# Two edits to DMA issue order in a fused spectral-filter and GEGLU kernel: the first gate weights move to ScalarE's queue, and the two returns of the third group part are issued together

## The chip, the core and the metric

The kernel runs on one core of a Trainium2 chip. The metric is device time in microseconds (us), the median over runs of the whole program. A profiled execution has a time of its own, and its trace covers a span a little shorter than that time.

## The reference

The input x has shape 1 x 2048 x 512 in bf16. It is normalised row by row, and two branches work on the result:

```python
xn = _layernorm(x, axis=-1)
return x + _A_ref(xn, A_w_r, A_w_i) + _B_ref(xn, B_w_gate, B_w_up, B_w_down)

# _A_ref: irfft2(rfft2(xn) * (w_r + 1j * w_i))          (2048 x 257 filter)
# _B_ref: (gelu(xn @ w_gate) * (xn @ w_up)) @ w_down     (512 -> 1792 -> 512)
```

## The kernel before

**Tiling.** The 2048 rows are held as 16 tiles of 128 rows by 512 columns. Row block b (0 to 3) is four tiles. Everything is on the chip at once: weights, filters and activations have their own SBUF buffers, and each engine has one list of instructions, written out by hand in program order by `sch.op`. An instruction waits on semaphores of what it depends on; an engine never goes past an instruction that waits. So the order of the calls at the end of the function is the order of each engine's work. A DMA is issued by the engine whose list holds it: `load(..., eng="sp")` puts it on SyncE (SP), `eng="act"` on ScalarE (ACT). In the profile, SP's DMAs run on queue q1 and ACT's on queue q10.

**GEGLU.** `geglu_unit(b, fc, a, w)` multiplies one 128-column slice of the gate weights (4 matmuls, line 547), then the same slice of the up weights (4 matmuls, line 547), applies gelu on ACT (line 559) and the product on VectorE (line 567). `down_unit` does the 14 matmuls of the down projection (line 593) for one tile and adds to x (line 604). These units are also the filler that is put between the steps of the spectral branch so that TensorE (PE) has work while the spectral branch waits for transfers.

**The start.** SP issues, in this order, tiles x0 and x1 (128 KB each, lines 363-364), the first piece of gate and up weights (384 KB each, `load_w(0)`, line 365: called wg0 and wu0 here), tiles x2 and x3, the second piece of gate and up weights (256 KB each, wg1 and wu1, line 368), and the rest. ACT's first instruction is the load of a 32 KB identity matrix (line 344). Then tiles 0 and 1 are normalised: on VectorE the statistics of tile 0 (lines 413, 414), those of tile 1, the reciprocal for tile 0 (line 423) and its normalisation (line 436), in that order; the square roots are on ACT (line 419). PE transposes the normalised tile with the identity (line 451), VectorE copies it back (line 457), and the first gate matmul follows.

**The spectral branch.** Its two FFT directions are matmuls with constant matrices. In the middle, the 32 frequency groups go through 16 units u of two groups: `unit_B(u)` transforms (line 695), `product(u)` applies the filter, `unit_c(u)` transforms back (line 726), ACT copies the result from PSUM to a buffer Vp (line 731), and SP stores it in the DRAM buffer stage_g (line 735, 128.5 KB). SP also issues, for each u, two 64 KB copies JX (line 703). The groups fall into four parts of four units. When a part is stored, `back(part, pq, eng)` (line 738, DMA at line 743) reads it back in another layout, in two returns pq = 0 and 1 of 256 KB each:

```python
if u in (9, 10, 13, 14, 17, 18):
    back(u // 4 - 2, (u - 9) % 4, "act")
```

So parts 0, 1 and 2 (the first three) are returned by ACT, one return in step u and the other in step u + 1; part 3 is returned by SP after the loop (line 911), when the last stores have landed. In step 18, `unit_c(14)` and `unit_c(15)` come before the second return of part 2. `unit_e(j)` (line 757), the first step of the last transform, waits for all eight returns (`spec["perm2"]`). Its PE instructions are behind the filler of line 912. After it, `unit_fin(j)` finishes each tile on PE, ACT, VectorE and GpSimd (POOL, lines 792 and 796), and SP stores it.

Of the kernel before, what the change touches and what calls it, by code (L numbers as in the profile page):

```python
# [17 lines left out]
P = 128  # L18
# [133 lines left out]
class _Sched:  # L152
# [14 lines left out]
    def total(self, stream):  # L167
        return (stream, self.stream_cnt[stream])
# [59 lines left out]
def bass_parallel_sum__spectral_gfnet__glu_gated_geglu__prompt_kernel(  # L228
# [11 lines left out]
    c_small = nc.inline_tensor(small_np, name="c_small")  # L240
# [9 lines left out]
    with ExitStack() as es:  # L250

        def sb(name, shape, dt=BF16):
            return es.enter_context(nc.sbuf_tensor(name, shape, dt))
# [13 lines left out]
        small = sb("small", [P, small_np.shape[1]])  # L267
# [30 lines left out]
        ident = small[:, 0:P]  # L298
# [40 lines left out]
        def load(stream, dst, src, eng="sp"):  # L339
            sch.op(eng, lambda e: e.dma_start(dst, src), stream=stream)  # L340
            return total(stream)


        ev_id = load("ident", small[:, 0:P], c_small.ap()[:, 0:P], eng="act")
        WPIECES = ((0, 384), (384, 640), (640, 896), (896, 1280), (1280, FF))
        ev_w = {}
        spec = {}
# [1 line left out]
        def load_w(i, which=(0, 1), eng="sp"):  # L349
            a, b = WPIECES[i]  # L350
            for q in which:
                dst, src = ((wg_sb, B_w_gate), (wu_sb, B_w_up))[q]
                name = "w%d%s" % (i, "gu"[q])
                load(name, dst[:, :, a:b], src[:, a:b].rearrange("(r p) f -> p r f", p=P), eng=eng)
                ev_w[i, q] = total(name)
# [4 lines left out]
                ev_x[j] = ev  # L360

        ev_x = {}
        for j in (0, 1):
            ev_x[j] = load("x%d" % j, x_sb[:, j, :], xv[:, j, :])
        load_w(0)
        for j in (2, 3):
            ev_x[j] = load("x%d" % j, x_sb[:, j, :], xv[:, j, :])
        load_w(1)
# [318 lines left out]
        def unit_B(u):  # L687
            s3 = u % 4
            slot, bdeps = ring_sp.alloc(2)

            def f_b(e):
                ins = None
                for i in range(2):
                    g = 2 * u + i
                    ins = e.matmul(sp_bank(slot + i)[:, 0:NK], BM[:, 1 if g == 0 else 0, :], Tp[:, g, :], start=True, stop=True)  # L695
                return ins

            ev_p = sch.op("pe", f_b, deps=[spec["perm1"], ev_small] + bdeps)
            spec["B_last"] = ev_p
            ev_Xc[u] = sch.op("act", lambda e: e.activation(Xc[s3], sp_pair(slot), ACT.Copy), deps=[ev_p] + Xc_readers[s3])  # L700
            ring_sp.add_reader(slot, ev_Xc[u], 2)
            for h in range(2):
                sch.op("sp", lambda e, h=h: e.dma_start(JX[s3][64 * h:64 * h + 64, :, :], Xc[s3][64 - 64 * h:128 - 64 * h, :, :]),
                       deps=[ev_Xc[u]] + JX_readers[s3], stream="jx%d" % s3)
            ev_JX[u] = total("jx%d" % s3)
            Xc_readers[s3] = [ev_JX[u]]

        def product(u):

            s2, s3 = u % 2, u % 4  # L710
            gs = slice(2 * u, 2 * u + 2)
            a = sch.op("dve", lambda e: e.tensor_tensor(M1[s2], Xc[s3], wr_sb[:, gs, :], ALU.mult), deps=[ev_Xc[u]] + M_readers[s2] + spec["wr"])
            b = sch.op("dve", lambda e: e.tensor_tensor(JX[s3], JX[s3], wi_sb[:, gs, :], ALU.mult), deps=[ev_JX[u], spec["neg"][u // 4]])
            ev_Y[u] = sch.op("dve", lambda e: e.tensor_tensor(M1[s2], M1[s2], JX[s3], ALU.add), deps=[a, b])
            Xc_readers[s3].append(a)
            JX_readers[s3] = [ev_Y[u]]

        def unit_c(u):
            s2, sv = u % 2, u % 3
            slot, bdeps = ring_sp.alloc(2)  # L720

            def f_c(e):
                ins = None
                for i in range(2):
                    kind = 1 if 2 * u + i == 0 else 0
                    ins = e.matmul(sp_bank(slot + i)[:, 0:NK], CM[:, kind, :], M1[s2][:, i, :], start=True, stop=True)  # L726
                return ins

            ev_p = sch.op("pe", f_c, deps=[ev_Y[u]] + bdeps)
            M_readers[s2] = [ev_p]  # L730
            ev_v = sch.op("act", lambda e: e.activation(Vp[sv][:], sp_pair(slot), ACT.Copy), deps=[ev_p] + Vp_readers[sv])  # L731
            ring_sp.add_reader(slot, ev_v, 2)
            part = next(i for i, (lo, hi) in enumerate(PARTS) if lo <= 2 * u < hi)
            name = "vd%d_%d" % (part, sv)
            sch.op("sp", lambda e: e.dma_start(d2[2 * u:2 * u + 2].rearrange("g r k -> r g k"), Vp[sv][:]), deps=[ev_v], stream=name)
            Vp_readers[sv] = [total(name)]

        def back(part, pq, eng):

            lo, hi = PARTS[part]  # L740
            src = bass.AP(tensor=d2.tensor, offset=d2.offset + (lo * P + 16 * pq) * NK + pq,
                          ap=[[32 * NK, 4 * (hi - lo)], [NK, NJ], [1, HD]])
            sch.op(eng, lambda e: e.dma_start(V[4 * lo:4 * hi, :, pq * HD:(pq + 1) * HD], src),
                   deps=[total("vd%d_%d" % (part, i)) for i in range(3)] + [spec["A_last"]], stream="perm2")
            spec["perm2"] = total("perm2")
# [104 lines left out]
        def filler(n=1):  # L850
            for _ in range(n):
                u = next(fill, None)
                if u is None:
                    return
                todo["left"] -= 1
                if u[0] == "g":
                    geglu_unit(u[1], u[2])
                else:
                    down_unit(u[1], u[2])
# [36 lines left out]
        for u in range(19):  # L896
            for v in ((14, 15) if u == 18 else (u - 4,)):
                if v >= 0:
                    unit_c(v)
            if u < 16:  # L900
                unit_B(u)
            for v in {15: (12, 13), 16: (14,), 17: (15,), 18: ()}.get(u, (u - 3,)):
                if v >= 0:
                    product(v)
            if 1 <= u < 18:
                filler()

            if u in (9, 10, 13, 14, 17, 18):
                back(u // 4 - 2, (u - 9) % 4, "act")
        for pq in range(2):  # L910
            back(3, pq, "sp")
        filler(todo["left"] - 15 - 2)
# [59 lines left out]
```

## Time and profile before

| what | us |
|---|---|
| median of 3 runs | 182.88 |
| lowest and highest run | 182.47, 183.36 |
| the profiled execution: its time | 182.96 |
| the profiled execution: its span | 181.2 |
| PE busy | 174.0 (96% of the span) |
| VectorE, ACT, POOL busy | 116.1, 87.4, 55.3 |
| granted TensorE clock | 1.0 throughout |

Times inside the profile are us from the start of the span. The 1.76 us between span and time lie outside of what the trace shows. A group of instructions is named by engine, line, operation and tile. SPq and ACTq are the issuing of DMAs by these engines; the time to landing of a DMA runs from its issue to its semaphore.

### The profile page before, as it was taken

Reading aid. Unit: us, or ns where it says so; the run is one execution under the profiler, and the core shown is the slowest. Engines: PE = TensorE matmul, PEld = TensorE weight load, DVE = VectorE, ACT = ScalarE, POOL = GpSimd, SP = SyncE. Lnnn points to the kernel's source line nnn. Section 1 sums busy time; section 2 is a strip of 40 time slices with the busy share of each in tenths; the row PEclk is TensorE's granted clock in tenths of the full one; section 3 lists DMA queues with packets and bytes.
Section 4 is the critical chain, followed back from the end, with each engine's and each line's share of the span. In section 5 each row is a group of like instructions: output and inputs, shape, how many; then the busy total and the mean of one; then the engine's idle time right before and its main releaser. Section 6 shows DMA issues by size and latency. Waiting matters only on the chain.

```text
span 181.2 us, 3209 instructions
## 1 busy us (share of the span) xinstructions
PE 174.0 (96%) x1163; PEld 98.1 (54%) x1163; DVE 116.1 (64%) x255; ACT 87.4 (48%) x164; POOL 55.3 (31%) x54
## 2 busy tenths in 40 slices
PE   7899999999999999999999999999799999999991
PEld 7678655555555544454554555454255555555550
DVE  3587977788765636537586858863336678873372
ACT  3744347776562533166374737362154366642300
POOL 0047262344560000000000000000006979995663
PEclk9999999999999999999999999999999999999999
DMA  5999999999997794813343866754500111111001
GB/s 136 324 339 381 373 358 167 182 183 225 219 200 196 151 271 141 261 36 84 92 122 83 195 154 134 188 92 113 119 0 29 55 35 58 58 60 62 31 29 58
DMA packets 37520, 27.15 MB, mean 150 GB/s; under 512 B 6656, under 2 KB 36736, under 8 KB 37376
## 3 DMA queue, kind: packets, MB, share of 16 engines
q1 hardware_dynamic: 34192, 25.34, 55.1%
q10 hardware_dynamic: 3312, 1.61, 4.8%
q8 instruction: 9, 0.15, 0.3%
q14 instruction: 7, 0.06, 0.2%
HBM read 17.48 MB, written 6.30 MB: 131 GB/s over the span
## 4 chain that ended last, share of the span: by engine, by line
PE 68%; POOL 13%; DMA 9%; DVE 3%; issue 3%; SPq 2%; POOLq 1%; ACT 1%; ACTq 0%; DVEq 0%
PE ps L547 41%; PE ps L593 17%; POOL x_sb L796 7%; POOL bufC L792 5%; DMA wu_sb<-in_B_w_up_dram 3%; DMA stage_g<-Vp 3%; DMA bufB<-stage_g 3%; PE ps L646 2%; PE ps L620 2%; PE ps L695 2%; PE ps L726 2%; SPq L340 2%; DVE bufC L789 1%; DVE bufC L788 1%; PE ps L757 1%
## 5 line engine op out<-in xcount | busy, mean ns | idle before, releaser
L547 PE MATMUL ps<-xnT,wu_sb 128*128 128x512 bf16 (+2 forms) x264 | 59.2, 347 | 0.4 <-DMA wu_sb<-in_B_w_up_dram 0.4
L547 PE MATMUL ps<-xnT,wg_sb 128*128 128x512 bf16 (+2 forms) x264 | 59.2, 347 | 0.4 <-DVE xnT L457 0.4
L567 DVE TENSOR_TENSOR hT<-ps,gg 128x512 bf16<-128x512 f32 (+2 forms) x66 | 39.5, 606 | 27.1 <-PE ps L547 25.3
L593 PE MATMUL ps<-wd_sb,hT 128*128 128x512 bf16 (+2 forms) x238 | 50.8, 366 | 0.0
L559 ACT ACTIVATE gg<-ps 128x512 bf16<-128x512 f32 (+2 forms) x66 | 35.1, 533 | 26.5 <-PE ps L547 22.7
L792 POOL TENSOR_TENSOR bufC<-bufC 128x256 bf16<-128x256 f32 x16 | 14.8, 922 | 89.9 <-DVE bufC L789 89.9
L547 PEld LDWEIGHTS ps<-xnT,wu_sb 128*128 128x128 bf16 x264 | 24.9, 98 | 24.6 <-DMA wu_sb<-in_B_w_up_dram 0.9
L593 PEld LDWEIGHTS ps<-wd_sb,hT 128*128 128x128 bf16 x238 | 22.4, 98 | 23.0
L547 PEld LDWEIGHTS ps<-xnT,wg_sb 128*128 128x128 bf16 x264 | 23.8, 98 | 15.2 <-issue 0.7
L604 DVE TENSOR_TENSOR x_sb<-ps,x_sb 128x512 bf16<-128x512 f32 (+2 forms) x17 | 11.1, 660 | 24.3 <-PE ps L593 16.0
L796 POOL TENSOR_TENSOR x_sb<-x_sb,bufC 128x512 bf16<-128x512 bf16 x16 | 18.7, 1170 | 2.3
L507 POOL TENSOR_TENSOR bufC<-bufA 128x1024 bf16<-128x1024 bf16 x8 | 16.8, 2125 | 8.5 <-DVE bufA L436 8.5
L762 ACT ACTIVATE bufA<-ps 128x512 bf16<-128x512 f32 x16 | 9.4, 597 | 17.2 <-PE ps L757 17.2
L731 ACT ACTIVATE Vp<-ps 128x514 bf16<-128x514 f32 x16 | 9.5, 600 | 15.3 <-PE ps L726 15.3
L654 ACT ACTIVATE bufB<-ps 128x512 bf16<-128x512 f32 x16 | 11.9, 745 | 9.5 <-PE ps L646 9.5
L413 DVE BATCH_NORM_STATS2 st<-x_sb 128x6 f32<-128x512 bf16 x16 | 10.9, 680 | 2.2 <-DMA x_sb<-in_A_x_dram 2.2
L788 DVE TENSOR_TENSOR bufC<-bufC,ps 128x256 f32<-128x256 f32 x16 | 6.7, 419 | 4.6 <-ACT bufC L785 4.6
L627 ACT ACTIVATE tmp<-ps 128x512 bf16<-128x512 f32 x9 | 5.4, 598 | 6.1 <-PE ps L620 6.1
L428 POOL TENSOR_SCALAR rstd<-ag 128x4 f32<-128x4 f32 (+1 forms) x4 | 1.3, 317 | 21.3 <-DVE ag L414 21.3
L700 ACT ACTIVATE Xc<-ps 128x514 bf16<-128x514 f32 x12 | 7.0, 595 | 1.0 <-PE ps L695 1.0
L757 PEld LDWEIGHTS ps<-fa,bufB 128*128 128x128 bf16 x64 | 4.8, 98 | 5.1 <-DMA bufB<-stage_g 1.8
L757 PE MATMUL ps<-fa,bufB 128*128 128x128 bf16 x64 | 6.0, 219 | 1.3 <-DMA bufB<-stage_g 1.3
(50 smaller groups left out, 138.2 us busy)
## 6 DMA issues: line engine op xcount, KB each, us to landing
stage_g<-Vp SPq DMA_DIRECT2D x16, 128.5 KB, 3.4
bufC<-stage_p SPq DMA_DIRECT2D x4, 512.0 KB, 5.2
out_dram<-x_sb SPq DMA_DIRECT2D x15, 128.0 KB, 1.7
wd_sb<-in_B_w_down_dram SPq DMA_DIRECT2D x1, 1792.0 KB, 14.6
stage_p<-bufB SPq DMA_DIRECT2D x7, 256.0 KB, 5.6
wr_sb<-in_A_w_r_dram SPq DMA_DIRECT2D x6, 257.0 KB, 10.5
wi_sb<-in_A_w_i_dram SPq DMA_DIRECT2D x6, 257.0 KB, 10.1
JX<-Xc SPq DMA_DIRECT2D x24, 64.2 KB, 2.4
```

The source lines that it names most:

```text
L413: ev = sch.op("dve", lambda e: e.bn_stats(st[:, j, :], x_sb[:, j, :]), deps=[ev_x[j]])
L507: ev_hf[m] = [sch.op("pool", lambda e, t=t, op=op: e.tensor_tensor(half[:, m, t, :, :], rows[:, 0, :, :], rows[:, 1, :, :], op), deps=deps ...
L547: ins = e.matmul(gu_bank(slot)[:, 0:w], wsb[:, dc, fc * P:(fc + 1) * P], xnT[:, dc, b * 512 + a:b * 512 + a + w], start=(dc == 0), stop=(d ...
L559: ev_gg = sch.op("act", lambda e: e.activation(gg, gu_bank(gslot)[:, 0:w], ACT.Gelu_apprx_tanh), deps=[ev_gm] + gg_readers[s2])
L567: ev_h = sch.op("dve", lambda e: e.tensor_tensor(hT[hb][:, fc, a:a + w], gu_bank(uslot)[:, 0:w], gg, ALU.mult), deps=[ev_um, ev_gg] + hdeps)
L593: ins = e.matmul(bank(slot)[:, 0:w], hT[hb][:, fc, jj * P:(jj + 1) * P], wd_sb[:, fc, cs], start=(fc == 0), stop=(fc == NFC - 1))
L604: ev_a = sch.op("dve", lambda e, slot=slot, cs=cs, w=w: e.tensor_tensor(x_sb[:, j, cs], bank(slot)[:, 0:w], x_sb[:, j, cs], ALU.add), deps ...
L654: ev_T[j] = sch.op("act", lambda e: e.activation(dst, src, ACT.Copy), deps=[ev_p])
L731: ev_v = sch.op("act", lambda e: e.activation(Vp[sv][:], sp_pair(slot), ACT.Copy), deps=[ev_p] + Vp_readers[sv])
L757: ins = e.matmul(sp_bank(slot)[:, ci * P:(ci + 1) * P], V[:, j, V0[ci]:V0[ci] + HD - 1:2], EM[:, j, :], start=True, stop=True)
L792: y = [sch.op(("dve", "pool")[h], lambda e, h=h, op=op: e.tensor_tensor(rS[s2][:, h * HD:(h + 1) * HD], yeS[s2][:, 0, :], yeS[s2][:, 1, :] ...
L796: ev_o = sch.op("pool", lambda e: e.tensor_tensor(x_sb[:, j, :], x_sb[:, j, :], rS[s2], ALU.add), deps=[a, b, ev_xn[j]] + ev_acc.get(j, []))
```

## The change

There are two edits. First, wg0 is issued by ACT as its first instruction, ahead of the identity, and is gone from SP's list; wu0 stays on SP and follows x1 directly. Second, both returns of part 2 are issued by ACT in step 17, one behind the other, instead of one in step 17 and one in step 18. The other returns stay where they were. No other instruction changes its place on its engine. The code below the first edit stands one line lower than before.

```diff
-        ev_id = load("ident", small[:, 0:P], c_small.ap()[:, 0:P], eng="act")
...
         ev_x = {}
+        load_w(0, (0,), eng="act")
+        ev_id = load("ident", small[:, 0:P], c_small.ap()[:, 0:P], eng="act")
         for j in (0, 1):
             ev_x[j] = load("x%d" % j, x_sb[:, j, :], xv[:, j, :])
-        load_w(0)
+        load_w(0, (1,))
...
-            if u in (9, 10, 13, 14, 17, 18):
-                back(u // 4 - 2, (u - 9) % 4, "act")
+            for pq in {9: (0,), 10: (1,), 13: (0,), 14: (1,), 17: (0, 1)}.get(u, ()):
+                back(u // 4 - 2, pq, "act")
```

## The prediction

> **What bounds the kernel now.** I read the page's busy times first, then PE's waits over the whole span, then the chain of waits around the two edits, and last the packets of each DMA queue in short windows.
>
> ```profile
> PE 174.0 (96%) x1163; PEld 98.1 (54%) x1163; DVE 116.1 (64%) x255; ACT 87.4 (48%) x164; POOL 55.3 (31%) x54
> ```
>
> PE is the bound. A change that leaves PE's instructions alone can only move where PE stands idle, so the list of PE's waits is the list of what there is to win:
>
> ```profile
> PE ps L757 <- DMA bufB<-stage_g: 1.3, 1, 1.3
> PE ps L527 <- DVE hT L407: 1.0, 1, 1.0
> PE ps L547 <- DMA wu_sb<-in_B_w_up_dram: 0.4, 2, 0.2
> PE ps L547 <- DVE xnT L457: 0.4, 1, 0.4
> PE ps L451 <- DVE rstd L423: 0.2, 1, 0.2
> ```
>
> The columns are total us, times, longest. One wait of 1.3 us is for the returns. Two waits of 0.2 us are for up weights at the start. The rest belongs to the start-up chain from tile 0. Between 13 and 130 us PE waits for nothing, so what shifts PE at the start shifts everything behind it. The chain of waits around the returns, in order of time (start, us, what):
>
> ```profile
> 120.57 0.56 ACT Vp L731
> ...
> 121.14 5.28 DMA stage_g<-Vp
> ...
> 126.43 0.33 SPq L743
> ...
> 126.81 4.58 DMA bufB<-stage_g
> ...
> 131.43 0.62 PE ps L757 x8
> ```
>
> The last store of stage_g takes 5.28 us to land; SP then issues the last two returns, and PE starts 4.6 us after that. PE's last filler ends at 130.15, hence 1.28 us idle. From 131.43 to the end PE, VectorE and POOL follow one another in PE's rhythm of 2.17 us a tile (1.73 + 0.22 + 0.22 in the chain), so an earlier start there is kept to the end.
>
> **Second edit (returns).** Why does that store take 5.28 us, when those issued at 93.33, 95.50 and 115.46 land in 2.7 to 2.8? Packets by queue (q1 is SP, q10 is ACT) in two windows, 120.2 to 122.8 and 122.8 to 125.2:
>
> ```profile
> q10 hardware_dynamic: 691, 0.35, 91.1%
> ```
>
> ```profile
> q1 hardware_dynamic: 544, 0.26, 41.9%
> q10 hardware_dynamic: 321, 0.16, 21.8%
> ```
>
> A return is 528 packets. The two last stores, issued at 120.65 and 121.14, move no packet until 122.8. At that point ACT has moved 796 - 528 = 268 packets of the second return, issued at 120.26. So a transfer on the other queue, if issued behind a return, starts when about half of the return has moved. The second return itself begins badly: from 121.2 to 121.6 the core moves 20 to 31 GB/s.
>
> After the edit ACT issues the second return at 119.26, right behind the first (118.95 to 119.26, 0.31 us an issue). It does not have to wait, since part 2's stores have landed by 116.8. Behind it on ACT are the two Vp copies, which wait for PE until 120.03; the second issue ends at 119.57, so it delays nothing. The first return is half through at 120.8, as now. The pair needs 528 packets more until it is half through its second. In 120.6 to 121.0 the returns move 189 packets, some 450 per us, so that point comes 1.15 us later, at 121.95. The stores then start 0.85 us sooner than 122.8, which moves PE's start up by as much. Bounds: PE's idle time caps the gain at 1.28 us. A store that met no return would take 3.0 us at most (91.16) and land at 124.1, well beyond the cap. At the other end, a slow first half (2.5 us from issue, as the second return had) puts the same point at 118.95 + 2.5 + 1.15 = 122.6, and only 0.2 is won. A loss is excluded, because no instruction comes later on any engine. I take 1.05, the middle between 0.85 and the cap: the last two returns on SP, issued 0.38 us apart (126.43 and 126.81), had moved 746 of 1056 packets 2.77 us after the first issue, here 121.7, so the point of 796 may come a little before 121.95.
>
> **First edit (weights).** What it removes: SP's issue of wg0, 0.43 us with its gap 0.47 us. wu0 and all of SP's later loads are issued 0.47 us sooner. What it can give is PE's two waits for up weights, 0.24 us at 6.84 and 0.18 at 10.31. The transposes of tiles 2 and 3 at 12.63 came ready within 0.1 us of PE, behind VectorE work that shares only the first gain, so I count 0.24 to 0.42 and take 0.35. ACT's list: the identity moves back by one issue, the table load of 1.28 us (now 1.18 to 2.46) ends some 0.4 us later, and the first square root at 4.06 covers it. The identity now queues behind 384 KB; wg0 on SP has all its packets through 3.1 us after issue, so on ACT by about 3.8, the identity lands before 5, and PE first needs it at 5.43. wg0 itself (now landing at 5.54, used at 6.21) comes sooner.
>
> What it costs is x0 and x1, which now share the start with 384 KB. VectorE's rows show when they are needed:
>
> ```profile
> 3.11 0.69 DVE L413 BATCH_NORM_STATS2 st<-x_sb 128x6 f32<-128x512 bf16 x1 [2.19 <-DMA x_sb<-in_A_x_dram]
> 3.84 0.18 DVE L414 BATCH_NORM_AGGREGATE ag<-st 128x2 f32<-128x6 f32 x1
> 3.94 0.66 DVE L413 BATCH_NORM_STATS2 st<-x_sb 128x6 f32<-128x512 bf16 x1
> ...
> 4.74 0.13 DVE L423 RECIPROCAL rstd<-rstd 128x1 f32<-128x1 f32 x1
> ```
>
> VectorE starts when x0 lands, and x1 (landing at 3.37) has until 3.9 before it too delays the reciprocal and with it the first matmul. The nearest row for an SP transfer beside a large ACT transfer is JX beside a return, ACT issue at 109.41, SP issue at 109.44 (windows 109.42 to 112.0, then 112.0 to 112.8):
>
> ```profile
> q10 hardware_dynamic: 278, 0.14, 44.4%
> q1 hardware_dynamic: 273, 0.13, 18.6%
> ```
>
> ```profile
> q10 hardware_dynamic: 232, 0.11, 53.0%
> q1 hardware_dynamic: 141, 0.10, 41.7%
> ```
>
> The 273 of q1 are an older store; JX has its first packet at 112.0, after 278 packets of the return, and lands in 4.0 us where 2.0 to 2.4 is usual. wg0 too is 528 packets. Half of them have moved 1.85 (first return of part 2) to 2.5 us (wg0 on SP, the return at 109.41) after the issue; from 0.73 that is 2.6 to 3.25.
>
> x1 is issued at 1.17, clearly behind wg0. It starts at 2.6 to 3.25, takes 0.8 us for its 136 packets beside wg0's second half (141 packets of q1 in 0.8 us above) and lands 0.55 us after the last, at 3.95 to 4.6. That is 0 to 0.7 us too late, and I take 0.35. x0 is issued at 0.72, wg0 at 0.73. If x0 goes first it lands as now; the edit then costs 0.35 and gives 0.35, sum 0 (-0.4 to +0.4).
>
> Sum: 182.96 (span 181.2 + 1.76) - 1.05 + 0 = 181.9. The median of the runs is 0.08 below the profiled time.
>
> **A rule against the first edit.** The rows above show no exchange of packets between the queues in the first half of a large transfer. The Trainium skill, "DMA: Bandwidth & Descriptors", section "Issuing engines are not separate DMA queues", says that DMAs from different engines run on the same 16 engines and interleave, so that issuing from several saves only issue time. As an estimate from that page, interleaving from the first packet on would put 104 KB of wg0 between x0's packets and as much again between x1's, about 0.3 us each at some 320 GB/s, which also ends near 181.9.
>
> **The rivals.** (1) x0 goes behind wg0. Its lead is 0.01 us, and now the identity, issued at 0.73, has 26 packets through before x0's second. Then x0 starts at 2.6 to 3.25, needs 0.8 and 0.55 and lands at 3.95 to 4.6 instead of 3.11. That is 0.85 to 1.5 us, middle 1.15, less 0.35: +0.8, and 182.96 - 1.05 + 0.8 = 182.7. For it speaks JX, 0.03 us behind a return; against it, that x0 is first by the issue rows. (2) Slower: x0 waits for all of wg0, not half. wg0 has its last packet 3.1 us after issue, at 3.8; x0 alone then needs 0.45 and 0.6 and lands at 4.85, 1.75 late. Less 0.35 that is +1.4, and 183.3; if the returns give only 0.2, 184.2. It decides from an x0 landing past 3.11 + 0.35 + 1.05 = 4.5. Against it: JX went through after half. (3) The second edit does not do what it says: the stores land as late as now for another reason, since the last packet at 125.1 precedes the landing by 1.3 us. Then 0 to 0.2 is won, and with x0 first the time is 182.9.
>
> **How the numbers follow.** The forecast has 0.53 (its own range 181.3 to 182.4), rival 1 has 0.29 (182.0 to 183.3), rival 2 has 0.10, rival 3 has 0.08. The range 181.2 to 183.5 leaves out the worse half of rival 2 and corners of the others. A measurement here tells about 0.5% from no change, 0.91 us, so faster means below 181.97. About 0.38 of the forecast's 0.53 lies there and 0.04 of rival 1. Slower means above 183.8: 0.07 of rival 2, 0.04 of rival 1's upper end with weak returns, 0.01 else. Faster 0.42, same 0.46, slower 0.12.
>
> **What would show it.** Right: q1 has its first store packets at about 122 in place of 122.8, the last store lands in under 4.5 us, and PE's wait at line 758 shrinks from 1.3 to under 0.4. At the start VectorE's first statistics begin near 3.1, the second near 4.2, and PE's waits for wu_sb are gone. Wrong: first statistics after 3.8 (rival 1) or 4.5 (rival 2), or a last store still near 5 us (rival 3).

## The result and the profile after

In this measurement the changed kernel is slower. Its median is 184.17 us (183.11 to 185.62, 13 runs) against 182.88 us (182.15 to 183.40, 13 runs) before. The ratio is 1.0073, with a 95% interval of 1.0044 to 1.0103. That is above the range's upper end of 183.5. The kernel was measured twice more in the experiments below (both_again, both_third), and there its medians, 182.25 and 182.24 us, lie inside the range and can't be told from the kernel before.

The profiled execution of the changed kernel took 183.5 us, with a span of 181.7 us (before: 181.2). Its busy times hardly differ from before, so the half microsecond in this execution is idle time of PE. All lines of the code below the first edit have moved down by one. PE's waits (total us, times, longest):

```profile
PE ps L758 <- DMA bufB<-stage_g: 1.0, 1, 1.0
PE ps L528 <- DVE hT L408: 1.0, 1, 1.0
PE ps L528 <- DVE rstd L424: 0.5, 1, 0.5
PE ps L548 <- DVE xnT L458: 0.4, 1, 0.4
```

The waits for wu_sb are gone, as forecast. The wait for the returns fell only from 1.3 to 1.0 us. The third line is new: PE's warm-up matmuls are over, and PE stands still until tile 0 is ready. VectorE's rows at the start show why (start, us, what, idle time before and its releaser):

```profile
3.20 0.69 DVE L414 BATCH_NORM_STATS2 st<-x_sb 128x6 f32<-128x512 bf16 x1 [2.29 <-DMA x_sb<-in_A_x_dram]
...
5.13 0.69 DVE L414 BATCH_NORM_STATS2 st<-x_sb 128x6 f32<-128x512 bf16 x1 [1.02 <-DMA x_sb<-in_A_x_dram]
```

x0 came in time (3.20; before 3.11). x1 did not. The second statistics start at 5.13 instead of 3.94, and the reciprocal, the normalisation and the first transpose stand behind them. The transposes of tile 2, after which PE no longer waits for this chain, start at 13.44 instead of 12.63. So 0.81 us of the 1.19 us is still there, and stays to the end. The chain of waits around the returns (start, us, what):

```profile
121.95 4.37 DMA stage_g<-Vp
...
126.34 0.33 SPq L744
...
126.71 5.20 DMA bufB<-stage_g
...
131.95 0.62 PE ps L758 x8
```

The last store landed in 4.37 us instead of 5.28, as the second edit intended. But the last returns themselves took 5.20 us instead of 4.58. PE starts line 758 at 131.95, before at 131.43: 0.52 us later, which is the difference of the spans: 0.81 us from the start, less some 0.3 us of wait.

What one profile does not show is the clock. The mean granted clock of the 13 runs of the changed kernel is under 0.992 in six (184.17 to 185.62 us) and from 0.995 to 1.0 in the other seven (median 183.5 us). Of the 122 runs of the kernel before that accompany the experiments, one is under 0.992.

### The profile page after: what moved, and what is told of

Its sections match the earlier page's. It is cut to its first block, busy times and chain, and to the rows that moved or that the text cites. A ratio compares the mean times of both kernels' runs of the same rounds, so it can differ in the third digit from the quotient of the medians.

```text
span 181.7 us, 3190 instructions
## 1 busy us (share of the span) xinstructions
PE 173.4 (95%) x1144; PEld 98.7 (54%) x1163; DVE 116.2 (64%) x255; ACT 87.3 (48%) x164; POOL 55.3 (30%) x54
## 4 chain that ended last, share of the span: by engine, by line
PE 67%; POOL 13%; DMA 7%; DVE 6%; issue 3%; ACT 1%; POOLq 1%; SPq 0%; DVEq 0%
PE ps L548 40%; PE ps L594 17%; POOL x_sb L797 7%; POOL bufC L793 5%; DMA bufB<-stage_g 3%; DMA stage_g<-Vp 2%; DMA x_sb<-in_A_x_dram 2%; PE ps L647 2%; PE ps L621 2%; PE ps L696 2%; PE ps L727 2%; DVE st L414 1%; DVE bufC L790 1%; DVE bufC L789 1%; PE ps L758 1%
## 5 line engine op out<-in xcount | busy, mean ns | idle before, releaser
L548 PE MATMUL ps<-xnT,wg_sb 128*128 128x512 bf16 (+2 forms) x254 | 57.5, 345 | 0.9 <-DVE xnT L458 0.4
L594 PE MATMUL ps<-wd_sb,hT 128*128 128x512 bf16 (+2 forms) x232 | 50.0, 366 | 0.3
L414 DVE BATCH_NORM_STATS2 st<-x_sb 128x6 f32<-128x512 bf16 x16 | 10.9, 682 | 3.3 <-DMA x_sb<-in_A_x_dram 3.3
L786 ACT ACTIVATE bufC<-ps 128x256 f32<-128x256 f32 x16 | 6.0, 378 | 2.6 <-PE ps L779 2.6
```

The source lines that it names most:

```text
L414: ev = sch.op("dve", lambda e: e.bn_stats(st[:, j, :], x_sb[:, j, :]), deps=[ev_x[j]])
L548: ins = e.matmul(gu_bank(slot)[:, 0:w], wsb[:, dc, fc * P:(fc + 1) * P], xnT[:, dc, b * 512 + a:b * 512 + a + w], start=(dc == 0), stop=(d ...
L594: ins = e.matmul(bank(slot)[:, 0:w], hT[hb][:, fc, jj * P:(jj + 1) * P], wd_sb[:, fc, cs], start=(fc == 0), stop=(fc == NFC - 1))
```

## The experiments

My first theory was: x1's late landing costs about 0.8 us, and a pause of PE that now follows the warm-up lets the clock drop in some executions. The rivals were ScalarE's queue itself (the issue, the later table load, the later identity) and the returns, which won less than forecast. Ratios are to the kernel before, run on the same chip in the same series, with 95% intervals.

### One edit at a time

weights_only has the first edit alone; the returns are as before:

```diff
-            for pq in {9: (0,), 10: (1,), 13: (0,), 14: (1,), 17: (0, 1)}.get(u, ()):
-                back(u // 4 - 2, pq, "act")
+            if u in (9, 10, 13, 14, 17, 18):
+                back(u // 4 - 2, (u - 9) % 4, "act")
```

> Only the first edit: wg0 on ScalarE as its first instruction, the returns as before. Theory T (x1 queues behind wg0, lands near 5.1 instead of 3.4, and PE's start-up chain is late by about 1.2 us less the 0.42 us of up-weight waits): slower than before by 0.8 us at least, near 184, with the second VectorE statistics starting near 5.1 and PE's wait for the returns still 1.3 us. Rival R1 (the returns edit is what costs): 182.9 to 183.1. Rival R2 (the late PE start also lets the TensorE clock drop in part of the runs, 3.4 us at half clock where it happens): 184 to 185, with a wide spread between runs and a mean granted clock near 0.988 in the slow ones.

Measured: 183.17 us (12 runs), ratio 1.0035 [1.0007, 1.0063]. Second statistics at 5.05, no wait for the returns (the theory had 1.3 us), one run of 12 with a low clock. The loss is 0.56 us, less than the 0.8 us expected.

returns_only has the second edit alone:

```diff
-        load_w(0, (0,), eng="act")
-        ev_id = load("ident", small[:, 0:P], c_small.ap()[:, 0:P], eng="act")
...
-        load_w(0, (1,))
+        load_w(0)
```

(with the identity back in its old place).

> Only the second edit: both returns of part 2 in step 17, weights as before. Theory T: the last stores start about 0.9 us sooner, PE's wait for the returns falls from 1.3 to between 0.2 and 0.9 us, and the time is 182.0 to 182.6, all runs at a granted clock over 0.995. Rival R1 (the returns edit is what costs): 183.4 or more, with PE's wait for the returns not shorter.

Measured: 181.83 us (12 runs), ratio 0.9957 [0.9940, 0.9975], 0.78 us faster than the 182.61 of the kernel before. All clocks are 0.996 or more. PE's waits in it, all of them:

```profile
PE ps L527 <- DVE hT L407: 1.0, 1, 1.0
PE ps L547 <- DVE xnT L457: 0.4, 1, 0.4
PE ps L476 <- DVE bufA L436: 0.2, 1, 0.2
PE ps L547 <- DMA wu_sb<-in_B_w_up_dram: 0.2, 1, 0.2
```

The wait for the returns is gone. So the second edit is a gain of 0.78 us and the first a loss of 0.56 us; in this series the medians of the two kernels lie 1.34 us apart. Their sum, -0.2 us, is not the +1.3 us that the first measurement showed for both.

### Is it ScalarE's queue, or x1's place?

x1_behind_wg0 is the kernel before with one swap in SP's list; nothing is on ScalarE that was not there:

```diff
-        for j in (0, 1):
-            ev_x[j] = load("x%d" % j, x_sb[:, j, :], xv[:, j, :])
-        load_w(0)
+        ev_x[0] = load("x0", x_sb[:, 0, :], xv[:, 0, :])
+        load_w(0, (0,))
+        ev_x[1] = load("x1", x_sb[:, 1, :], xv[:, 1, :])
+        load_w(0, (1,))
```

> The kernel before, with nothing on ScalarE but the identity; only SyncE's order is x0, wg0, x1, wu0 instead of x0, x1, wg0, wu0. Theory T (the lateness of x1 alone costs, wherever it queues): x1 lands near 5 and the time is 183.5 to 185, like the first edit alone. Rival R3 (what costs is ScalarE: its longer issue, its later table load, or its queue): 182.9, with x1's lateness hidden. With R2 the spread between runs is wide here too.

Measured: 184.14 us (12 runs), ratio 1.0064 [1.0033, 1.0094]; second statistics at 5.47, seven of 12 runs with clocks of 0.986 to 0.991. x1 behind wg0 on one queue costs at least as much as the first edit, without ScalarE having a part in it. That falls in with the packets of the changed kernel (queue, packets, MB, share; q1 is SP, q10 ACT) in the windows 1.6 to 3.4, 3.4 to 3.8 and 3.8 to 4.0:

```profile
q10 hardware_dynamic: 252, 0.19, 42.4%
q1 hardware_dynamic: 144, 0.13, 28.6%
```

```profile
q10 hardware_dynamic: 174, 0.13, 98.3%
q1 hardware_dynamic: 3, 0.00, 2.2%
```

```profile
q10 hardware_dynamic: 68, 0.05, 71.4%
q1 hardware_dynamic: 29, 0.03, 41.7%
```

The 144 packets of q1 are x0 (136) and a few more. wg0 has moved 252 of 528, its half, at 3.4, but x1 gets almost nothing until 3.8, when 426 have moved. From then on it is quick. It is no accident of one execution: in all eight profiles in which ScalarE issues wg0 as one load, the second statistics start between 4.96 and 5.19.

wg0_split keeps both edits and cuts wg0 into two loads of 264 packets each, in the same place on ScalarE:

```diff
-        load_w(0, (0,), eng="act")
+        for h in range(2):
+            load("w0g", wg_sb[:, 2 * h:2 * h + 2, 0:384],
+                 B_w_gate[256 * h:256 * h + 256, 0:384].rearrange("(r p) f -> p r f", p=P), eng="act")
+        ev_w[0, 0] = total("w0g")
```

> The changed kernel with wg0 on ScalarE as two loads of 264 packets in place of one of 528. If a load on the other queue has to wait until only some 16 packets per DMA engine of the one ahead are left, the first half holds x1 up for almost nothing and x1 goes before the second half: x1 lands at 3.6 to 4.2 instead of 5.1, second statistics below 4.3, and the time falls to 181.6 to 182.4. If ScalarE's queue simply goes first or takes its share by bytes, x1 lands near 5 as in the changed kernel.

Measured: 182.02 us (12 runs), ratio 0.9969 [0.9951, 0.9987]; the unsplit version of the same series (both_again, below) has 182.25. Its packets from 2.9 to 3.8 are

```profile
q10 hardware_dynamic: 229, 0.16, 56.2%
q1 hardware_dynamic: 139, 0.13, 43.7%
```

x1 now moves beside wg0, and the second statistics start at 4.69, not below 4.3 as expected. x0 is later (first statistics at 3.66), and PE now waits 0.4 us for the identity, which is behind both pieces. The 0.23 us between the two medians are not clear of the noise.

x1_on_act has the second edit, x1 as ScalarE's first instruction in place of wg0, and wg0 back on SP:

```diff
-        load_w(0, (0,), eng="act")
+        ev_x[1] = load("x1", x_sb[:, 1, :], xv[:, 1, :], eng="act")
         ev_id = load("ident", small[:, 0:P], c_small.ap()[:, 0:P], eng="act")
-        for j in (0, 1):
-            ev_x[j] = load("x%d" % j, x_sb[:, j, :], xv[:, j, :])
-        load_w(0, (1,))
+        ev_x[0] = load("x0", x_sb[:, 0, :], xv[:, 0, :])
+        load_w(0)
```

> The returns edit stays; the start is turned round: ScalarE issues x1 and then the identity, SyncE x0, wg0, wu0. No small load is behind a large one on the other queue. Theory T: x1 lands by 3.6, first statistics near 3.1 and second near 3.9, wu0 and wu1 come up to 0.4 us sooner than in returns_only: 181.4 to 181.9. Rival (any load on ScalarE's queue beside SyncE's at the start costs): 182.4 or more.

Measured: 181.72 us (6 runs), ratio 0.9943 [0.9921, 0.9965], all clocks 0.995 or more. The two small loads share the engines from the start, so the first statistics start at 3.60 and the second at 4.42, each 0.5 us later than expected. The gate and up weights keep PE waiting nowhere. It is faster than both kernels. Against returns_only, measured elsewhere at 0.9957, it can't be told apart.

### The clock

Before tile 0, PE does 42 matmuls of zeros as a warm-up, and 3 more when tile 0's reciprocal is there; line 25 has their numbers. warm_54 is the changed kernel with

```diff
-NWARM = (42, 3)
+NWARM = (54, 3)
```

> The changed kernel with 54 instead of 42 matmuls that keep PE busy before tile 0 is ready. If R2 holds (PE's pause before the late tile lets the clock drop or rise late), the slow runs go: spread under 1.3 us, granted clock over 0.994 in all, time 182.9 to 183.6. If the lateness of x1 is all, the time stays near 184.2 with the spread of the changed kernel, or is later by up to 0.4 us where the longer warm-up itself ends after tile 0 is ready.

Measured: 182.51 us (12 runs), ratio 0.9991 [0.9971, 1.0011], no run under 0.995. The time is below the expected range, but x1 is as late as ever (5.19).

both_again is the changed kernel once more:

> The changed kernel once more, so that it stands beside the others on one chip. If the edits only add, it is weights_only (+0.55 us against before) plus returns_only (-0.8), near 182.4, with the wide spread of weights_only. If it is again 1.0 to 1.4 us above before, the two edits do not add, and the part of runs with a granted clock near 0.988 should be larger than the 1 in 12 of weights_only.

Measured: 182.25 us (12 runs), ratio 0.9990 [0.9965, 1.0014]. Nine runs with clocks of 0.995 to 1.0 took 182.04 to 182.41 us. Three at 0.990 to 0.991 took 183.44, 183.52 and 183.73. The profiled execution is one of the three. PE's longest wait in it, and its stretches 4.1 to 7.5 and 7.5 to 10.9 (length, then busy us and instructions of PE, PEld, VectorE, ACT and POOL, granted clock, DMA share, GB/s):

```profile
PE ps L528 <- DVE rstd L424: 1.2, 1, 1.2
```

```profile
4.10:7.50 3.40, 1.69 (x23) 1.22 (x21) 1.91 (x9) 1.69 (x3) 0.00 (x0) 1.00 1.13 335
7.50:10.90 3.40, 3.40 (x34) 3.39 (x35) 1.26 (x5) 1.86 (x7) 0.00 (x0) 0.51 1.17 323
```

The same stretches of warm_54:

```profile
4.10:7.50 3.40, 2.31 (x35) 1.85 (x33) 1.85 (x8) 1.62 (x3) 0.00 (x0) 1.00 1.13 330
7.50:10.90 3.40, 3.40 (x57) 3.26 (x58) 2.33 (x9) 2.58 (x10) 0.00 (x0) 1.00 1.17 323
```

After 7.5 PE is busy throughout in both, but at a clock of 0.51 it gets 34 matmuls done where 57 are possible. The stretch at half clock lasts 3.4 us and ends by itself. It costs the 1.4 us by which the three runs are longer than the nine (183.52 - 182.15, medians). What precedes it is a pause: in both_again the warm-up ended at 5.0, 1.15 us before tile 0 was ready; in warm_54 0.53 us before. Chance comes in with the start of the full rate. In the profile of the changed kernel PE does 12 matmuls from 4 to 5 us, in both_again 16, so there the same 42 ended 0.6 us sooner and the pause was longer by as much (1.15 against 0.51).

The Trainium skill, "TensorE: Matmul & The Clock Gate", section "HAM oscillation — how this bites in real kernels", gives as its rule that PE should have no idle gaps above about 3.4 us. By it, a pause of 1.2 us would be harmless here. The rows above show otherwise, and the measurement decides.

Of the 17 profiles of this case, three show the drop: both_again, x1_behind_wg0 and both_warm30. There PE was busy for 1.70, 1.53 and 1.28 us in the 3.4 us before it. In the 14 others the emptiest 3.4 us between 3.4 and 8.7 hold 2.05 us (wg0_split) or more. The longest single pause does not tell them apart: the kernel before stands still for 1.28 us at 130.15 and keeps its clock, with 2.12 us of work in the 3.4 us around it. So in these profiles it is the sum over some 3.4 us that does, and the dividing line lies between 1.7 and 2.05 us, about a half. Nothing was run to test that line by itself.

If the warm-up's length decides, it must do so in the kernel before too, and a shorter one must make the drop common. before_warm54 and before_warm30 are the kernel before with 54 and 30 in line 25, both_warm30 is the changed kernel with 30.

> The kernel before with 54 instead of 42 matmuls ahead of tile 0. If a longer warm-up helps only where tile 0's chain is late, it costs here: tile 0's reciprocal is ready near 4.9 us, and 54 matmuls at some 107 ns end near 6.7 if the clock has not risen by then: 182.6 to 183.6. If it is a gain by itself, whatever the loads do, 181.9 to 182.3 with a narrow spread; then the gain of warm_54 says nothing of x1.

> Both edits with 30 matmuls ahead of tile 0 instead of 42: PE then pauses for 1.9 us or more before the late tile in every run, not in some. If that pause is what drops the clock, most runs have a granted clock near 0.988 or rise late, and the median is 183.3 or more, against 182.25 for 42. If the clock drop has nothing to do with the pause, the share of such runs stays at a quarter to a half and the median between 182.2 and 184.2 as for 42.

> The kernel before with 30 matmuls ahead of tile 0. x1 is in time, so PE pauses for 0.6 us (clock not yet up) to 1.3 us only. If the length of PE's pause sets the share of dropped clocks, this has fewer than both_warm30 (5 of 7 at 0.991): at most a third, median 182.4 to 183.3. If the number of matmuls sets it, most runs drop here too and the median is 183.5 or more.

Measured: before_warm54 182.11 us (12 runs), ratio 0.9977 [0.9958, 0.9997], no low clock. I expected a cost; it gained 0.53 us, and why stays open. both_warm30 183.42 us (7 runs), ratio 1.0051 [1.0032, 1.0069], four of seven runs at 0.991 (not five, as the expectation of before_warm30 has it); in its profile PE pauses 1.8 us. The other three took 183.18, 183.39 and 184.17 us, no less than the four. before_warm30 182.74 us (12 runs), ratio 1.0008 [0.9981, 1.0036], four of 12 at 0.991. So in either kernel the warm-up's length bears on how often the clock drops: with 30 in eight of 19 runs, with 54 in none. With 42 the kernel before has one low clock in 122 runs, and x1's 1.2 us use up what it had in hand.

A clock that reads 1.00 is not always full speed, though. In the profile of before_warm30 the stretches 8 to 9 and 9 to 10 are

```profile
8.00:9.00 1.00, 1.00 (x13) 1.00 (x11) 0.04 (x1) 0.88 (x3) 0.00 (x0) 1.00 1.19 304
9.00:10.00 1.00, 1.00 (x20) 1.00 (x18) 0.55 (x3) 0.47 (x2) 0.00 (x0) 1.00 1.22 299
```

PE is busy throughout and does matmuls of one shape, but from 8 to 9 it does 13, as in both_again at a clock of 0.50 (12). So the column shows a drop after full speed was reached, but not that full speed was reached late, and a run with a mean clock near 1.0 may have lost time in this way.

### With the clock kept up

Three kernels with 54 warm-up matmuls, run together, take the drop of the clock out: returns_warm54, weights_warm54 and both_warm54 (the second edit, the first, and both).

> The returns edit with the weights as before, and 54 matmuls ahead of tile 0. The returns should give what they gave without the longer warm-up, up to 1.28 us, and the longer warm-up 0.5 as in before_warm54: 181.0 to 181.5, or 1.1 to 1.6 below before. If the two overlap (the warm-up only hides where the returns' wait already was), it stays at returns_only's -0.8.

> The first edit alone with 54 matmuls, so that the clock stays up in the late start. If the lateness of x1 costs by itself, this is slower than before_warm54 (0.5 below before) by the 0.4 to 0.8 us that PE starts late: 0.0 to 0.3 above before. If the price of the first edit is the clock alone, it is as fast as before_warm54.

> Both edits with 54 matmuls, beside its two parts on one chip. Against returns_warm54 it shows the price of the first edit with the clock kept up: 0.4 to 0.8 us slower if x1's lateness costs, equal if not.

Measured, 12 runs each: 181.76 us, ratio 0.9967 [0.9950, 0.9984]; 182.42 us, 0.9997 [0.9984, 1.0010]; 182.38 us, 0.9981 [0.9959, 1.0002]. None of the 36 runs has a low clock. Beside the second edit, the first costs 182.38 - 181.76 = 0.62 us without any drop of the clock. Beside the first edit, the second gives 0.04 us, which is nothing. returns_warm54 is 0.82 us below the kernel before, as much as returns_only, so the gains of the longer warm-up and of the second edit do not add.

### The last two

both_third is the changed kernel again; x1_on_act_warm48 is x1_on_act with 48 warm-up matmuls.

> The changed kernel a third time: 13 runs had a median of 184.17 (6 of them with a granted clock under 0.99), 12 later ones 182.25 (3 of 12 at 0.99). If the clock drop and slow returns come by chance in each execution, this lies between, 182.2 to 184.2, and its runs fall into a group at full clock and one some 1.4 us above with a clock near 0.99. If every run at full clock is again at 183.1 or more, something of the place it ran on adds about 1 us that the clock does not show.

> The returns edit, x1 on ScalarE ahead of the identity, and 48 matmuls ahead of tile 0: a version meant to beat both. If the late clock rise still costs x1_on_act (0.92 below before), this is 1.0 to 1.3 below before with a spread under 0.7 us; if 48 matmuls end after tile 0 is ready and only hold it up, 0.6 to 0.9 below.

Measured: both_third 182.24 us (12 runs), ratio 1.0008 [0.9978, 1.0037], one run with a low clock (183.34); two at 0.998 and 1.0 took 183.47 and 184.65 us all the same, which the groups expected by clock do not cover. x1_on_act_warm48 181.66 us (12 runs), ratio 0.9965 [0.9946, 0.9985]. It is 0.89 us below the kernel before of its series, as x1_on_act is 0.92 below that of its own. Six warm-up matmuls more change nothing that these runs show. Whether a late full rate costs x1_on_act anything stays open.

## Why the prediction was wrong, point by point

**First edit, what it gives (0.35): right.** PE's waits for wu_sb, 0.42 us together, are gone in all profiles with this edit.

**First edit, what it costs (0.35): right in kind, far off in size.** The step that failed reads "x1 ... starts at 2.6 to 3.25", when half of wg0 has moved. x0 did go first, so rivals 1 and 2 were not the reason (first statistics at 3.20, where they needed 3.8 or 4.5), though rival 2 was near in having a load wait for all of wg0. x1 waited for 426 of the 528 packets, not 264, and landed at 5.11 instead of 3.95 to 4.6.

The rule of the half was misread from the trace of before. At 122.8 ACT had moved 735 packets, not 796 (that is the count at 123.0), and the stores had only just begun. From 122.8 to 123.2 the queues moved

```profile
q10 hardware_dynamic: 180, 0.09, 75.1%
q1 hardware_dynamic: 14, 0.01, 6.1%
```

So the stores moved in earnest only from 123.2, when 915 of the returns' 1056 packets had gone, that is 387 of the second return's 528. The half stood for the first packets only.

The delay of the second statistics is 1.19 us where the sum had 0.35. With the 0.42 us gained, 0.81 is left at 13.44, and 0.62 to 0.8 us is what the edit costs on balance by the runs (both_warm54 against returns_warm54; spans of weights_only and returns_only, 180.4 and 179.6). The sum of the edit was about +0.7, not 0.

**A term that was not in the sum: the clock.** I read PE's granted clock as 1.0 throughout, though in before, too, PE does 12 matmuls from 3 to 4 us and 22 from 8 to 9, and did not ask what PE did while tile 0 became later. The 42 warm-up matmuls are there for that time, and in the profile of before they ended with no pause ahead of tile 0's reciprocal. A step that makes the first tile 1.2 us later makes PE's pause longer by up to as much, which had to be priced. It costs about 1.4 us in a share of the executions: six of 13, three of 12 and one of 12 in three measurements of the same kernel.

**The weighed rule.** The Trainium skill, "DMA: Bandwidth & Descriptors", section "Issuing engines are not separate DMA queues", would have x1 and wg0 interleave. Here they did not (3 packets of x1 beside 174 of wg0), while x1 and x0, 128 KB each, did in x1_on_act (120 packets of ACT beside 149 of SP from 1.7 to 2.9). Those two were issued at the same moment, 0.72, and x1 0.44 us behind wg0; whether the size or the order of issue makes the difference was not tried.

**Second edit (-1.05): right in direction; the size was that of one execution.** Alone it gives 0.78 us (returns_only). The 1.28 us of PE's idle time, its cap, belonged to the execution that was profiled. Of the profiles with the old returns, x1_behind_wg0 has 0.9, and weights_only, before_warm54, weights_warm54 and before_warm30 have none. The store that took 5.28 us was a slow one, too: in those five profiles the last store lands in 4.26 to 4.56 us, and in the eleven with the new returns in 3.71 to 4.56. The kernel before runs from 181.36 to 183.35 us in the series of returns_only, whose fastest run is 181.43: it looks as if the edit takes away the slower executions and leaves the fastest as they were. In the profile after, the forecast signs came in part: the last store under 4.5 us (4.37), but the pair of returns moved 545 packets from 121.6 to 123.2, some 340 per us where I had put 450, the stores moved in earnest only from 123.4, after 906 of the returns' 1056 packets where I had put 796, and the last returns were 0.6 us slower. Half of the second return was too early a point here too. The time that rival 3 had, next to no gain, is what weights_warm54 and both_warm54 show (0.04); for the second edit alone it is refuted.

**What stays open.** The changed kernel measured 184.17 us the first time and 182.25 and 182.24 us later. So most of the distance between the first median and the forecast did not come back, and the cost of x1 explains the rest of the miss, not this part. The clock as the profile shows it accounts for part of the 1.9 us only: the runs at 0.995 and more have medians of 183.5, 182.15 and 182.24 us, and a late full rate, which that number does not show, may play into each of them. The two profiles at such clocks differ by 1.0 us in the wait for the returns (1.0 and none, spans 181.7 and 180.3), so the landing of the last returns may be it. One profile of each cannot settle that. That two of three medians lie in the forecast's range is luck as far as the first edit goes: its term was about 0.7 us off. Why the second edit gives little once PE is late was not tried either.

## What to carry to other kernels

Before moving a large load to an idle queue, list the small loads that are issued within the next microsecond, and assume that they wait for most of it, as x1 did here. What should go to the second queue first is the small load that the first result waits for. A large load in pieces let the small one through, but gave no time that is clear of the noise. When a change delays the first real matmul, compare the end of the warm-up with the new start and lengthen it, and look at the granted clock of many runs, since one profile shows only one outcome. A wait that is to be won should be seen in more than one execution before it is priced.

## What was not expected of the hardware

- A 384 KB load of 528 packets holds back a 128 KB load issued 0.44 us later on the other queue until 81% of it (426 packets) has moved. As two loads of 264 packets it lets the other through (139 packets beside 229). Two loads of 128 KB, issued at the same moment, share from the start.
- A pause of 1.2 us, 5 us after the start, brought the granted clock to 0.5 for 3.4 us. The three profiles with a drop have at most 1.70 us of PE work in the 3.4 us before it, the 14 without have at least 2.05. A pause of 1.28 us at 130.15 in before, with 2.12 us of work in 3.4, left the clock as it was.
- The clock column reads 1.00 also where PE has not yet reached its full rate: 13 matmuls from 8 to 9 us in before_warm30, 20 from 9 to 10.
- The landing of the last returns differs between executions of one kernel by enough to make PE wait 1.0 us or not at all.
